# A buffer of its own for the small group's output in a fused attention and MLP kernel

## The chip, the cores and the metric

The kernel runs on one core of a Trainium2 chip. The metric is the device time of one execution in microseconds (us), median of several runs. The engines are named as the profile names them: PE is the matmul engine (PEld its weight loads), DVE the vector engine, ACT the scalar engine, POOL GpSimd, and SP the sync engine, which here issues DMA transfers only.

## The reference

```python
def _attn_ref(x, inducing):              # x: 4 x 12480 x 128, inducing: 32 x 128
    ...
    def mab(q, kv):
        s = scale * (q @ kv.transpose(0, 2, 1))
        s = s - s.max(-1, keepdims=True)
        a = np.exp(s)
        a /= a.sum(-1, keepdims=True) + 1e-09
        return a @ kv
    h = mab(I, x)                        # 32 rows per batch
    return mab(x, h)

def _moe_ref(x, w_in, w_out):            # 49920 x 128, 128 x 2048, 2048 x 128
    h = x @ w_in
    relu6 = np.clip(h + 3.0, 0.0, 6.0)
    g = h * relu6 / 6.0
    return g @ w_out
```

The output is `_moe_ref` of the attention's output, 49920 rows of 128 float32.

## The kernel before, in words

There are four batches b of 12480 tokens. Each is cut into groups: six of 2048 tokens (128 partitions times TG = 16) and a small last one of 192 tokens (96 partitions times 2). A large group has four chunks of 512 tokens, the small group is one chunk of 192: 25 chunks per batch (NCK), 100 in all. Phase a reads a batch's tokens and forms the 32 aggregated rows H. Phase c turns H into coefficients: since each token's attention output is a mix of the 32 rows of H, the first MLP matmul and the gate become products of attention weights, and the output is a linear part (BD) and a quadratic part (Cq). Phase b applies them to each chunk.

The order of the work is written out by hand. The main loop (from L970) goes over the 100 chunks t. For each it emits, in this order: the evacuation of the chunk before (`b_evac`), the spread of weights for the chunk six ahead (`b_spread`, an SP transfer into d), the product TD = TF * d for the next chunk (`b_prod`, L845, DVE), the first half of the features two chunks ahead (`b_base`, L827 on PE into bp, L834 on ACT into TF), at a group's turn its sum and nf (`b_f`, L751 on PE, L753 on DVE), the linear matmul that opens the chunk's PSUM bank op (`b_lin`, L856), then four rounds of quadratic matmuls from TF and TD into op (`b_quad`, L875). Between the rounds come the reciprocals r (`b_r`, L783 on PE, L787 on DVE), the packed weights of later groups (`b_pack`, L799 and L806; `b_e`, L735 and L741), and `bg`, which takes units of phases a and c of the next batch from a queue sorted by planned times. These units end with batch 3, which has no next batch. Among them are `a_T` (transposes L290, copy to xT L291), `a_s1` (L298 on PE, L304 on ACT), `a_agg` (L314 on PE, L327 on DVE, and the next load of x, L132 on POOL's queue), and `c_dG` on POOL (L516 waits for the newest TD, then L518 and L519).

`b_evac` (L884 to L902) multiplies op by r into an output buffer os (L892, DVE). At a group's first chunk (j == 0) it takes a new buffer from the pool osp, which has two (L107); when the group is full, SP writes it to DRAM in one transfer (L902), 1 MB for a large group. In the last two groups of the last batch each chunk is written by itself (L900). A buffer taken a second time waits until the write out of it has landed. op has two banks (psO), and the other matmuls share five banks (psF), so a matmul that needs a bank waits for its last reader.

The pool cst has one buffer per name or tag (L108). Its tag scr is used for d32 (L590) and r6 (L540), both before the first chunk of batch 0, and for junk in `count` (L950), which DVE runs in the last six chunks: `counts` at t == total - 6 (L1009), then L1011, and at t == total - 1 L988. Each is 2048 bytes per partition or less.

Of the kernel before, what the change touches and what calls it, by code (L numbers as in the profile page):

```python
# [9 lines left out]
FP32 = mybir.dt.float32  # L10
# [14 lines left out]
TG = 16  # L25
# [25 lines left out]
def kernel(  # L51
# [9 lines left out]
    P = nc.NUM_PARTITIONS  # L61
    B, N, C = x.shape
# [29 lines left out]
    with ExitStack() as es:  # L92
# [14 lines left out]
        osp = es.enter_context(tc.tile_pool(name="osp", bufs=2))  # L107
        cst = es.enter_context(tc.tile_pool(name="cst", bufs=1))  # L108
# [139 lines left out]
        def slots(n):  # L248

            return min(n, SL), max(n // SL, 1)  # L250
# [633 lines left out]
        def b_evac(b, c, op):  # L884
            g, j = chunks[c]
            t0, p, n = groups[g]
            st = S[b]
            if j == 0:
                st["os"] = osp.tile([P, TG, C], FP32, name="os")
            ot = st["os"]  # L890
            S_ = slots(n)[0]
            nc.vector.tensor_mul(  # L892
                ot[:p, j * S_ : (j + 1) * S_, :],
                op[:p, : S_ * C].rearrange("p (s c) -> p s c", c=C),
                r_all[:p, b, c, :S_].unsqueeze(2).to_broadcast([p, S_, C]),
            )
            r0 = b * N + t0
            rows = out[r0 : r0 + p * n, :].rearrange("(p i) c -> p i c", i=n)
            if b == B - 1 and g >= NGR - 2:
                nc.sync.dma_start(rows[:, j * S_ : (j + 1) * S_, :], ot[:p, j * S_ : (j + 1) * S_, :])  # L900
            elif (j + 1) * S_ == n:
                nc.sync.dma_start(rows, ot[:p, :n, :])  # L902
# [67 lines left out]
        for t in range(total):  # L970
# [4 lines left out]
            if evac:  # L975
                b_evac(*evac)
                evac = None
# [38 lines left out]

        assert not queue
        b_evac(*evac)
        verdict()

# [153 lines left out]
```

## Time and profile before

| | |
|---|---|
| median of three runs | 309.59 us |
| lowest and highest run | 309.18 and 311.05 us |
| the profiled execution | 310.18 us |
| its span, from the first to the last instruction | 308.3 us |
| mean granted PE clock in it | 0.987 |
| waits of SP's queue in L902 for os, total | 81.2 us in 25 waits |
| 1 MB writes of the output (23 of them), median to landing | 4.1 us |

A row of a timeline has the start in us from the span's start, the duration in us, the engine (SPq is SP's queue), the line, the operation, the tiles as out<-in, shapes as partitions x elements, the count of merged instructions, and in brackets the engine's idle time before it with the releaser that the profile infers. A row of waits has the waiting instruction, the releaser, total us, times, and the longest in us. A wait for several semaphores is put down to the one that came last by the profile; where that one had long been done, it was another, often a DMA. PE's matmuls are pipelined, so their modelled durations overlap, and distances between starts say more than durations.

### The profile page before, as it was taken

The page shows a single profiled execution, that of the slowest core. Times are in us where ns is not written, and L with a number is a line of the kernel's source. Part 1 is how long each engine was busy: PE and PEld are TensorE (multiplying, and loading weights), DVE is VectorE, ACT ScalarE, POOL GpSimd, SP SyncE. Part 2 cuts the span into 40 slices and gives each one's busy share as a digit, 9 for nine tenths or more (in the row PEclk, how much of TensorE's full clock was granted, in tenths as well). Part 3 has the DMA queues.
Part 4 walks back from the last instruction along what each step waited for, and adds up shares of the span by engine and source line. Part 5 has one row for each costly group of instructions (what it writes and reads, how often), then busy time and mean ns, then how long its engine had stood idle before and what let it go on. Part 6 is the DMA issues. An engine that isn't in the chain of part 4 may idle for free. (4 is left out here: it accounts for less than half of the span.)

```text
span 308.3 us, 9788 instructions
## 1 busy us (share of the span) xinstructions
PE 288.8 (94%) x3942; PEld 230.3 (75%) x3963; DVE 234.3 (76%) x499; ACT 224.9 (73%) x431; POOL 117.4 (38%) x234
## 2 busy tenths in 40 slices
PE   8978989999999899999998999998898999999992
PEld 3876577989888678777887977786687777777881
DVE  1567757887998578678897859788877885988893
ACT  3662769776968989668798899665696787777760
POOL 8460852431019995010097745000577760000000
PEclk9989999999999999999999999999999999999997
DMA  6999779699965547979628425256445565576753
GB/s 218 423 288 323 199 253 373 210 378 307 361 204 163 194 151 228 393 225 291 223 57 308 164 64 179 95 159 198 157 135 139 179 197 184 177 235 216 214 205 120
DMA packets 27441, 67.73 MB, mean 220 GB/s; under 512 B 5216, under 2 KB 20352, under 8 KB 21504
## 3 DMA queue, kind: packets, MB, share of 16 engines
q1 hardware_dynamic: 18784, 38.36, 38.4%
q0 software_dynamic: 8608, 28.71, 31.0%
q8 instruction: 32, 0.52, 0.7%
q14 instruction: 17, 0.14, 0.1%
HBM read 29.77 MB, written 25.56 MB: 179 GB/s over the span
## 5 line engine op out<-in xcount | busy, mean ns | idle before, releaser
L834 ACT ACTIVATE TF<-bp 128x512 bf16<-128x512 f32 (+1 forms) x200 | 115.6, 589 | 33.4 <-PE bp L827 17.9
L875 PE MATMUL op<-Cq,TF 128*128 128x128 bf16 (+1 forms) x784 | 104.7, 221 | 0.3
L875 PE MATMUL op<-Cq,TD 128*128 128x128 bf16 (+1 forms) x784 | 102.5, 219 | 0.0
L892 DVE TENSOR_TENSOR os<-op,r_all 128x512 f32<-128x512 f32 (+1 forms) x100 | 67.4, 674 | 23.5 <-PE op L875 18.9
L845 DVE TENSOR_TENSOR TD<-TF,d 128x1024 bf16<-128x1024 bf16 (+1 forms) x100 | 75.6, 756 | 4.3 <-ACT TF L834 3.3
L875 PEld LDWEIGHTS <-TF 128*128 128x128 bf16 (+1 forms) x784 | 55.1, 98 | 24.1 <-issue 12.7
L827 PE MATMUL bp<-xT,W 128*128 128x512 bf16 (+1 forms) x184 | 68.6, 375 | 2.2 <-DVE nf_all L753 1.0
L875 PEld LDWEIGHTS <-TD 128*128 128x128 bf16 (+1 forms) x784 | 60.3, 98 | 0.7 <-issue 0.2
L856 PE MATMUL op<-BD,nf 128*128 128x512 f32 (+1 forms) x100 | 52.3, 523 | 0.2 <-DVE os L892 0.2
L279 ACT CAST xb<-xr 128x512 bf16<-128x512 f32 (+1 forms) x70 | 45.3, 661 | 8.2 <-DMA xr<-in_x_dram 8.1
L291 DVE COPY xT<-pt 128x1024 bf16<-128x1024 bf16 (+1 forms) x56 | 34.0, 616 | 16.7 <-PE pt L290 15.8
L519 POOL TENSOR_TENSOR dg<-G 128x256 f32<-128x256 f32 x48 | 40.1, 836 | 0.0
L518 POOL TENSOR_TENSOR dg<-G 128x256 f32<-128x256 f32 x48 | 31.3, 653 | 14.6 <-ACT sq L526 10.1
L516 POOL COPY gate<-TD 128x1 bf16<-128x1 bf16 x48 | 11.7, 244 | 62.3 <-DVE TD L845 61.6
L526 ACT ACTIVATE sq<-dg 128x512 bf16<-128x512 f32 x48 | 30.3, 633 | 2.9 <-POOL dg L519 2.9
L314 PE MATMUL hnd<-xr,a 128*32 128x128 f32 x384 | 31.8, 229 | 0.6 <-ACT a L304 0.6
L290 PE MATMUL pt<-ident_b,xb 128*128 128x128 bf16 x392 | 30.9, 222 | 0.0
L603 PE MATMUL cp<-w_out_b,sq 128*128 128x128 bf16 x256 | 24.7, 219 | 2.5 <-ACT TF L834 1.3
L314 PEld LDWEIGHTS hnd<-xr,a 128*32 128x32 f32 x384 | 25.5, 111 | 1.7 <-ACT a L304 0.7
L783 PE MATMUL rp<-one,nf 128*128 128x4 f32 (+1 forms) x100 | 26.2, 264 | 0.5 <-ACT TF L834 0.5
L290 PEld LDWEIGHTS <-xb 128*128 128x128 bf16 x392 | 24.1, 99 | 2.8 <-issue 1.3
L806 ACT ACTIVATE dk<-pp 128x512 bf16<-128x512 f32 (+1 forms) x28 | 15.6, 556 | 12.3 <-PE pp L799 11.3
(127 smaller groups left out, 384.5 us busy)
## 6 DMA issues: line engine op xcount, KB each, us to landing
xr<-in_x_dram POOLq DMA_DIRECT2D x23, 1024.0 KB, 7.7
out_dram<-os SPq DMA_DIRECT2D x23, 1024.0 KB, 4.1
d<-dk SPq DMA_DIRECT2D x96, 128.0 KB, 4.4
xr<-in_x_dram POOLq DMA_DIRECT2D x2, 512.0 KB, 4.7
w_in_r<-in_moe_w_in_dram POOLq DMA_DIRECT2D x2, 512.0 KB, 10.7
w_out_r<-in_moe_w_out_dram POOLq DMA_DIRECT2D x1, 1024.0 KB, 14.1
out_dram<-os SPq DMA_DIRECT2D x4, 256.0 KB, 3.5
w_in_b<-in_moe_w_in_dram POOLq DMA_DIRECT2D x1, 512.0 KB, 7.7
```

The lines of the kernel that those rows point to most:

```text
L279: eng(xb[:p, lo:hi, :], xs[(b, g)][:p, lo:hi, :].bitcast(FP32))
L290: nc.tensor.transpose(pt[:, (i - lo) * p : (i - lo + 1) * p], xb[:p, i, :], ident_b[:p, :p])
L291: nc.vector.tensor_copy(st[("xT", g)][:, lo * p : hi * p], pt[:, : (hi - lo) * p])
L314: nc.tensor.matmul(st["hnd"][:M, :C], lhsT=a1[:p, i * M : (i + 1) * M], rhs=xs[(b, g)][:p, i, :], start=(g == 0 and i == 0), stop=(g == NG ...
L518: nc.gpsimd.tensor_sub(dg[:, 0], stepped(G2, jb, 0, 1, 0), stepped(G2, jb, 2, 0, 2))
L519: nc.gpsimd.tensor_sub(dg[:, 1], stepped(G2, jb, 1, -1, 0), stepped(G2, jb, 10, 0, 2))
L827: nc.tensor.matmul(bp[:, :w], lhsT=st["W"][:, k].rearrange("p m i -> p (m i)"), rhs=st[("xT", g)][:, j * w : (j + 1) * w],)
L834: nc.scalar.activation(st[("x", c)][:, k, :w], bp[:, :w], ACT.Exp, scale=scale)
L845: nc.vector.tensor_mul(u[:, :, :w], t[:, :, :w], d[:, :w].unsqueeze(1).to_broadcast([P, 2, w]))
L856: nc.tensor.matmul(op[:p, : S_ * C], lhsT=st[("nf", g)][:R, j * p : (j + 1) * p], rhs=st["BD"][:R, : S_ * C], start=True, stop=False, skip ...
L875: nc.tensor.matmul(op[:p, s * C : (s + 1) * C], lhsT=T[k][:, s * p : (s + 1) * p], rhs=st["Cq"][:, k, :], start=False, stop=(s == S_ - 1 a ...
L892: nc.vector.tensor_mul(ot[:p, j * S_ : (j + 1) * S_, :], op[:p, : S_ * C].rearrange("p (s c) -> p s c", c=C), r_all[:p, b, c, :S_].unsquee ...
```

## The change

The small group's output no longer takes a turn of the pool osp. It takes a tile of [128, 2, 128] float32, 1024 bytes per partition, in the pool cst under the tag scr, which it shares with d32, r6 and junk. The large groups go on taking turns of osp. The tile's name in the profile is ol.

```diff
             t0, p, n = groups[g]
             st = S[b]
             if j == 0:
-                st["os"] = osp.tile([P, TG, C], FP32, name="os")
+                if n == TG:
+                    st["os"] = osp.tile([P, TG, C], FP32, name="os")
+                else:
+                    st["os"] = cst.tile([P, n, C], FP32, name="ol", tag="scr")
             ot = st["os"]
```

## The prediction

> **What bounds the kernel now.** I read the page first, then DVE's waits, and then the timelines of DVE, SP and PE around the three places where a batch's small group is followed by the next batch. From the page:
>
> ```profile
> span 308.3 us, 9788 instructions
> PE 288.8 (94%) x3942; PEld 230.3 (75%) x3963; DVE 234.3 (76%) x499; ACT 224.9 (73%) x431; POOL 117.4 (38%) x234
> ```
>
> The reader is to see that PE is busy for 288.8 of 308.3 us. DVE, whose waits the change alters, idles 74 us, nearly all of it hidden: a wait on DVE is worth only what PE loses by it. DVE's waits have two entries that stand out because each is one occurrence alone:
>
> ```profile
> DVE os L892 <- PE rp L783: 2.2, 1, 2.2
> DVE os L892 <- PE pp L799: 1.8, 1, 1.8
> ```
>
> Columns are total us, times, longest. The named releasers can't be the true ones: an evacuation of op into os needs neither rp nor pp. So I looked at what else was due. First the end of batch 0 (DVE and one ACT row, then SP; the last two rows are the landing of that one SP transfer, and DVE's semaphore wait on L892):
>
> ```profile
> 129.02 0.69 DVE L291 COPY xT<-pt 128x1024 bf16<-128x1024 bf16 x1
> 129.46 0.60 ACT L834 ACTIVATE TF<-bp 128x512 bf16<-128x512 f32 x1 [0.51 <-PE bp L827]
> 131.92 0.69 DVE L892 TENSOR_TENSOR os<-op,r_all 128x512 f32<-128x512 f32 x1 [2.21 <-PE rp L783]
> 132.53 0.68 DVE L845 TENSOR_TENSOR TD<-TF,d 128x1024 bf16<-128x1024 bf16 x1
> 133.13 0.68 DVE L753 CUSTOM_DVE_ANT_0 nf<-e,sp 128x512 fp32r<-128x512 f32 x1
> ...
> 125.14 0.34 SPq L902 DMA_DIRECT2D out_dram<-os  x1
> ...
> DMA to landing us min/median/max: 6.7/6.7/6.7
> ...
> L892 DVEq EVENT_SEMAPHORE  x1: 50/50/50, 131.8 to 131.8; - x1
> ```
>
> The 1 MB write of batch 0's group 5 is issued at 125.14 and lands 6.7 later, at 131.8. That is when DVE's semaphore is passed, and 0.1 later the first os of batch 1 starts. The small group had taken the other buffer, so batch 1 needs group 5's at once. DVE stood still for 2.21 us with work queued behind: the TD product and the nf reduction.
>
> **The change part by part.** No arithmetic, shape, transfer or issue order changes. The small group's buffer comes from the one-buffer tag scr, so the two os buffers turn six times per batch instead of seven, and batch b+1's group 0 gets the buffer of batch b's group 4.
>
> *Removed, batch 0 to 1.* What PE lost:
>
> ```profile
> 126.53 0.38 PE L827 MATMUL bp<-xT,W 128*128 128x512 bf16 x1
> 126.98 0.28 PE L875 MATMUL op<-Cq,TF 128*128 128x128 bf16 x2
> 127.10 0.28 PE L875 MATMUL op<-Cq,TD 128*128 128x128 bf16 x2
> ...
> 128.93 0.28 PE L875 MATMUL op<-Cq,TD 128*128 128x128 bf16 x2
> ...
> 132.08 0.38 PE L827 MATMUL bp<-xT,W 128*128 128x512 bf16 x1
> 132.67 0.49 PE L856 MATMUL op<-BD,nf 128*128 128x512 f32 x1 [0.21 <-DVE os L892]
> 133.00 0.29 PE L875 MATMUL op<-Cq,TF 128*128 128x128 bf16 x2
> 133.27 0.28 PE L875 MATMUL op<-Cq,TD 128*128 128x128 bf16 x2
> 133.87 0.55 PE L298 MATMUL s<-I_T,xT 128*128 128x32 bf16 x16 [0.32 <-DVE nf_all L753]
> ...
> 198.28 0.28 PE L875 MATMUL op<-Cq,TD 128*96 128x128 bf16 x2
> 198.40 0.55 PE L298 MATMUL s<-I_T,xT 128*128 128x32 bf16 x16
> ```
>
> Undisturbed, L827 to the first TF matmul (past L856) takes 126.98 - 126.53 = 0.45, TF to TD 127.10 - 126.98 = 0.12, and TD to L298 198.40 - 198.28 = 0.12: together 0.69. Here 132.08 to 133.87 takes 1.79. PE waited for the op bank that os frees, then for TD (133.27, just after TD's end at 132.53 + 0.68 = 133.21), then for the bank that nf frees (133.13 + 0.68 = 133.81). All three are queued behind the stalled os, so the stall costs PE 1.79 - 0.69 = 1.10 us.
>
> What is late next? The os needs the op whose last matmul is done at 128.93 + 0.28 = 129.21, and DVE is free at 129.02 + 0.69 = 129.71; so it can start 131.92 - 129.71 = 2.21 earlier. TD then starts near 130.3; its TF is ready at 129.46 + 0.60 = 130.06. So PE's own instruction stream is what ends last there, and I take the whole 1.10. Its other end is zero, if something else fills the same place.
>
> *Removed, batches 1 to 2 and 2 to 3:*
>
> ```profile
> 202.13 0.28 PE L875 MATMUL op<-Cq,TD 128*128 128x128 bf16 x2
> 202.49 0.69 DVE L892 TENSOR_TENSOR os<-op,r_all 128x512 f32<-128x512 f32 x1 [0.56 <-PE op L875]
> ...
> 257.72 0.34 SPq L902 DMA_DIRECT2D out_dram<-os  x1
> ...
> DMA to landing us min/median/max: 4.0/4.0/4.0
> ...
> 261.84 0.69 DVE L892 TENSOR_TENSOR os<-op,r_all 128x512 f32<-128x512 f32 x1 [1.83 <-PE pp L799]
> ...
> 262.67 0.58 PE L856 MATMUL op<-BD,nf 128*128 128x512 f32 x1
> 264.47 0.50 PE L856 MATMUL op<-BD,nf 128*128 128x512 f32 x1
> 266.15 0.58 PE L856 MATMUL op<-BD,nf 128*128 128x512 f32 x1
> ...
> 270.26 0.58 PE L856 MATMUL op<-BD,nf 128*128 128x512 f32 x1
> 271.83 0.58 PE L856 MATMUL op<-BD,nf 128*128 128x512 f32 x1
> 273.48 0.58 PE L856 MATMUL op<-BD,nf 128*128 128x512 f32 x1
> ```
>
> Batch 2's first os starts at 202.49; its matmuls end at 202.13 + 0.28 = 202.41. It could start at most 0.08 earlier: nothing. Batch 3's waits for the write issued at 257.72 (257.72 + 4.0 = 261.7) and stalls 1.83. Batch 3 has no background work, so its groups repeat. Chunks 2 and 3 of group 0 take 264.47 - 262.67 = 1.80 and 266.15 - 264.47 = 1.68; those of group 1 take 271.83 - 270.26 = 1.57 and 273.48 - 271.83 = 1.65. PE lost 0.23 + 0.03 = 0.26.
>
> *Added.* The small os now waits for the last user of scr: in batch 0 for work finished before the first chunk, in batches 1 and 2 for a write one batch old, and in batch 3 for the counts' junk on DVE itself. The last is the only close one; it stands at the end of the kernel, with nothing queued behind but the last write:
>
> ```profile
> 302.24 0.28 PE L875 MATMUL op<-Cq,TD 128*96 128x128 bf16 x2
> ...
> 302.36 0.08 DVE L951 DVE_READ_ACCUMULATOR junk<-r_all 128x1 f32 x1
> 302.55 0.42 DVE L892 TENSOR_TENSOR os<-op,r_all 96x256 f32<-96x256 f32 x1
> ```
>
> The junk is done at 302.44, the matmuls at 302.52, so the wait is covered by 0.08 us. Uncovered, it costs about what lies between a semaphore passed and the next start, 0.1 us in the row at 131.8 and 131.92; a gain is excluded, since the matmuls come last anyway. I take 0. SP and POOL issue the same transfers in the same order; they only move earlier with the work.
>
> *Sum.* 1.10 + 0.00 + 0.26 = 1.36 us. The profiled execution took 310.18, so 308.82 on its scale. The median of the runs, 309.59, lies 0.59 below it: 309.59 - 1.36 = 308.23. I say 308.2.
>
> [...] What made the first stall long is the landing time, 6.7 against 4.0 us for the same 1 MB. The transfer engines were full there (columns: us; busy by engine; clock; DMA share and GB/s):
>
> ```profile
> 126.00:132.00 6.00, 5.93 (x81) 4.83 (x82) 3.54 (x9) 4.78 (x10) 0.18 (x1) 1.00 1.00 371
> ```
>
> [...] The row has 6.7 with every engine busy, and I go by the row.
>
> **The rivals.**
>
> *A. The write lands early.* If 6.7 us is a crossing of loads peculiar to the profiled execution, and other executions have the 4.0 of batch 2's end, it lands at 125.14 + 4.0 = 129.1, before 129.71, and the first stall isn't there. Only 0.26 is left: 309.59 - 0.26 = 309.3. Against it: the order of issue is fixed and the share is 1.00.
>
> *B. The gain is absorbed.* ACT (73%) and POOL pace stretches of batches 1 and 2; PE that comes earlier may wait there instead. Then some 0 to 0.5 us are left: 309.3. Against it: ACT's and POOL's work is released by PE's and DVE's own progress, and moves with it.
>
> *C. Slower: DVE's work falls against POOL's.*
>
> ```profile
> 236.88 0.61 POOL L518 TENSOR_TENSOR dg<-G 128x256 f32<-128x256 f32 x1 [0.51 <-ACT sq L526]
> 236.97 1.08 DVE L845 TENSOR_TENSOR TD<-TF,d 128x1024 bf16<-128x1024 bf16 x1
> ```
>
> A TD product beside POOL's dg takes 1.08 instead of 0.68 (132.53), 0.40 more. A shifted phase may stretch more of them in batches 1 and 2. It decides once 4 more stretched ones (1.6) lie on PE's path; with 8, the time is 309.59 - 1.36 + 3.2 = 311.4. [...] Against it: DVE has slack there, and as many may part as meet.
>
> *D. The change doesn't do what it says*, and the first os of a batch still waits for a write: 309.6.
>
> **How the numbers follow.** Chances: forecast 0.58, A 0.10, B 0.22, C 0.06, D 0.04. About 1% (3.1 us) is what a measurement of this kernel can tell from no change; only C with 11 or more stretched products on the path passes that upwards, and only a gain more than twice the sum downwards. So faster by over 1% 0.03, within 1% 0.94, slower 0.03. The range: the lowest run shown is 0.4 below the median, and the gain may be 0.6 larger if PE's lead spares a later stall: 307.2. Upwards it takes in A, B and D at 309.6 with 0.6 of scatter: 310.2. It leaves out most of C. The forecast's own range is 307.6 to 308.9.
>
> **What would show it.** In the changed trace DVE's two lone waits of 2.2 and 1.8 are gone; the small os carries a name of its own; the first os of batches 1 and 3 starts as soon as DVE is free; L827 to L298 after batch 1's second chunk takes near 0.7; chunk 2 of batch 3 takes 1.57. If these hold and the span is not about 1.4 shorter, B is right, and PE's idle time must be found later. If the landing is near 4 in the trace after, A gains. If more TD products take over 1 us than now, C does. The prediction is wrong if the stalls go and PE's steps there stay as they are.

## The result and the profile after

| | before | after |
|---|---|---|
| median | 309.63 us (308.82 to 311.52, 8 runs) | 307.75 us (307.58 to 309.0, 8 runs) |
| ratio | | 0.9936, 95% interval 0.991 to 0.9963 |
| profiled execution and its span | 310.18 and 308.3 us | 307.74 and 306.0 us |

The kernel became 0.6% faster, within the 1% named in the prediction; the interval leaves out 1, and a second series further down gives the same ratio. The ratio of `twice` further down leaves out two of its four runs, which took over 1.5% longer than its fastest. The medians differ by 1.88 us, the two profiled executions by 2.44, and the prediction was 1.36. So there are two questions: whether the 1.36 us came from where the prediction put them, and where the rest comes from.

The page after, its first two lines:

```profile
span 306.0 us, 9804 instructions
PE 286.6 (94%) x3963; PEld 228.6 (75%) x3963; DVE 235.0 (77%) x499; ACT 224.8 (73%) x431; POOL 117.2 (38%) x234
```

DVE's waits after (waiting line and releaser, total us, times, longest):

```profile
DVE os L895 <- PE op L875: 20.0, 55, 1.0
```

L895 is L892 of before, three lines further down. The two lone entries of 2.2 and 1.8 us are gone, and this is the only entry of os that is left. DVE's timeline at the start of batch 1 and of batch 3:

```profile
128.03 0.69 DVE L291 COPY xT<-pt 128x1024 bf16<-128x1024 bf16 x1
128.64 0.68 DVE L895 TENSOR_TENSOR os<-op,r_all 128x512 f32<-128x512 f32 x1
129.24 0.68 DVE L845 TENSOR_TENSOR TD<-TF,d 128x1024 bf16<-128x1024 bf16 x1
129.83 0.68 DVE L753 CUSTOM_DVE_ANT_0 nf<-e,sp 128x512 fp32r<-128x512 f32 x1
...
256.96 0.37 DVE L895 TENSOR_TENSOR ol<-op,r_all 96x256 f32<-96x256 f32 x1
257.25 0.68 DVE L845 TENSOR_TENSOR TD<-TF,d 128x1024 bf16<-128x1024 bf16 x1
258.23 0.69 DVE L895 TENSOR_TENSOR os<-op,r_all 128x512 f32<-128x512 f32 x1 [0.31 <-PE op L875]
```

The first os of batch 1 now follows the copy before it at once, TD and nf follow it, and batch 3's waits only for its own matmuls. PE's timeline after:

```profile
128.51 0.40 PE L856 MATMUL op<-BD,nf 128*128 128x512 f32 x1
131.09 0.38 PE L827 MATMUL bp<-xT,W 128*128 128x512 bf16 x1
131.12 0.58 PE L856 MATMUL op<-BD,nf 128*128 128x512 f32 x1
131.54 0.29 PE L875 MATMUL op<-Cq,TF 128*128 128x128 bf16 x2
131.66 0.28 PE L875 MATMUL op<-Cq,TD 128*128 128x128 bf16 x2
131.78 0.38 PE L298 MATMUL s<-I_T,xT 128*128 128x32 bf16 x9
133.79 0.58 PE L856 MATMUL op<-BD,nf 128*128 128x512 f32 x1
...
258.48 0.40 PE L856 MATMUL op<-BD,nf 128*128 128x512 f32 x1
260.58 0.59 PE L856 MATMUL op<-BD,nf 128*128 128x512 f32 x1
262.16 0.58 PE L856 MATMUL op<-BD,nf 128*128 128x512 f32 x1
263.80 0.59 PE L856 MATMUL op<-BD,nf 128*128 128x512 f32 x1
```

From L827 to L298 it takes 131.78 - 131.09 = 0.69 us, where the kernel before took 1.79: 1.10 less. In batch 3, chunk 2 takes 1.58 and chunk 3 1.64 instead of 1.80 and 1.68: 0.26 less. Both are what the prediction worked out. From the first chunk on, all other chunks keep their distances within 0.03 us. So 1.36 of the 2.3 us between the spans lie at the two stalls. Most of the rest lies ahead of the first chunk, where the change touches nothing: its L856 starts at 47.17 us before and at 46.21 after, 0.96 us apart. In this view of 4 us (busy time by engine in the order PE, PEld, DVE, ACT, POOL; the last three columns are the granted clock, the DMA share and GB/s) before comes first and after second:

```profile
20.00:24.00 4.00, 3.88 (x58) 3.85 (x59) 3.02 (x7) 2.16 (x4) 0.30 (x1) 0.59 1.43 192
```

```profile
20.00:24.00 4.00, 3.62 (x74) 3.52 (x75) 3.42 (x8) 2.95 (x6) 0.41 (x1) 1.00 1.43 187
```

The reader is to see the granted clock: 0.59 in the profiled execution before, 1.00 in the one after.

### The profile page after: what moved, and what is told of

The parts are those of the page before. It is cut to its first block, busy times and chain, and to the rows that moved or that the text cites. A ratio compares the mean times of both kernels' runs of the same rounds, so it can differ in the third digit from the quotient of the medians.

```text
span 306.0 us, 9804 instructions
## 1 busy us (share of the span) xinstructions
PE 286.6 (94%) x3963; PEld 228.6 (75%) x3963; DVE 235.0 (77%) x499; ACT 224.8 (73%) x431; POOL 117.2 (38%) x234
## 5 line engine op out<-in xcount | busy, mean ns | idle before, releaser
L895 DVE TENSOR_TENSOR os<-op,r_all 128x512 f32<-128x512 f32 x96 | 65.9, 686 | 20.7 <-PE op L875 20.0
L827 PE MATMUL bp<-xT,W 128*128 128x512 bf16 (+1 forms) x200 | 74.8, 375 | 2.2 <-DVE nf_all L753 1.0
L856 PE MATMUL op<-BD,nf 128*128 128x512 f32 (+1 forms) x100 | 52.5, 525 | 0.0
L314 PE MATMUL hnd<-xr,a 128*32 128x128 f32 x384 | 31.0, 226 | 0.6 <-ACT a L304 0.6
L290 PEld LDWEIGHTS <-xb 128*128 128x128 bf16 x392 | 23.3, 98 | 3.8 <-ACT xb L279 2.1
L314 PEld LDWEIGHTS hnd<-xr,a 128*32 128x32 f32 x384 | 24.7, 109 | 1.8 <-ACT a L304 0.7
```

The costliest lines, as they stand in the source:

```text
L290: nc.tensor.transpose(pt[:, (i - lo) * p : (i - lo + 1) * p], xb[:p, i, :], ident_b[:p, :p])
L314: nc.tensor.matmul(st["hnd"][:M, :C], lhsT=a1[:p, i * M : (i + 1) * M], rhs=xs[(b, g)][:p, i, :], start=(g == 0 and i == 0), stop=(g == NG ...
L827: nc.tensor.matmul(bp[:, :w], lhsT=st["W"][:, k].rearrange("p m i -> p (m i)"), rhs=st[("xT", g)][:, j * w : (j + 1) * w],)
L856: nc.tensor.matmul(op[:p, : S_ * C], lhsT=st[("nf", g)][:R, j * p : (j + 1) * p], rhs=st["BD"][:R, : S_ * C], start=True, stop=False, skip ...
L895: nc.vector.tensor_mul(ot[:p, j * S_ : (j + 1) * S_, :], op[:p, : S_ * C].rearrange("p (s c) -> p s c", c=C), r_all[:p, b, c, :S_].unsquee ...
```

## The experiments

For each profile below, the loss at batch 1 is measured in one way. In PE's timeline I take the distance of L856 of batch 1's second chunk to L856 of its fourth, and subtract that of the changed kernel, 133.79 - 128.51 = 5.28 us. For batch 3 it is the distance from its third to its fifth chunk, less 263.80 - 260.58 = 3.22.

**The kernel before once more** (no edit).

> The kernel before, unchanged, profiled once more. The two profiled executions before and after differ by 0.98 us already ahead of the first chunk's output matmul (47.17 against 46.21 us), where the change touches nothing, and in the first one the granted clock was 0.59 between 20 and 24 us. Theory: that part belongs to the execution and not to the kernel; in this trace it will be another amount (0 to 1 us), the granted clock between 20 and 24 us another, while every distance from the first chunk on is the same within 0.05 us, the 1.10 and 0.26 us losses at batches 1 and 3 among them. Rival: the first 47 us of the kernel before are slower by 1 us in every execution, so something in the change shortens them; then the first chunk's matmul starts at 47.2 again. Time: same, ratio 1.000 within 0.003.

Measured: 310.61 us (309.63 to 312.33, 11 runs), ratio 1.0035 (1.0014 to 1.0057). The same program, timed against itself, lies 0.35% off, outside the 0.3% that was expected, and its interval leaves out 1: single intervals of this size don't decide. Its mean clock was 0.993 or more in 1 of 11 runs, against 23 of the 35 beside it. Rows of its PE and DVE timelines and of two windows:

```profile
46.35 0.59 PE L856 MATMUL op<-BD,nf 128*128 128x512 f32 x1
128.68 0.40 PE L856 MATMUL op<-BD,nf 128*128 128x512 f32 x1
134.61 0.58 PE L856 MATMUL op<-BD,nf 128*128 128x512 f32 x1
...
130.65 0.69 DVE L892 TENSOR_TENSOR os<-op,r_all 128x512 f32<-128x512 f32 x1 [1.76 <-DMA out_dram<-os]
...
20.00:24.00 4.00, 3.53 (x73) 3.36 (x72) 3.34 (x8) 2.95 (x6) 0.84 (x2) 1.00 1.43 187
222.60:226.10 3.50, 3.50 (x25) 2.82 (x25) 1.50 (x3) 2.13 (x4) 2.24 (x6) 0.51 0.43 96
```

The first chunk starts at 46.35, not at 47.17, so at least 0.82 of the 0.96 us ahead of it belong to the execution, as expected. This execution was granted half the clock later, at 222.6 to 226.1, and lost 1.3 us there. And here the profile names the true releaser of batch 1's wait, the write out of os. One part of the expectation was wrong: the loss at batch 1 is not fixed. The distance is 134.61 - 128.68 = 5.93, a loss of 0.65 where the first profile had 1.10. The write landed 6.2 us after its issue, not 6.7, and DVE waited 1.76 us, not 2.21.

**One batch at a time.** `own_b0` gives only batch 0's small group the buffer of its own, `own_b2` only batch 2's.

```diff
-                if n == TG:
+                if n == TG or b != 0:      # own_b2: b != 2
```

> Only batch 0's small group gets the buffer of its own. Theory: the two stalls are separate, so the step at batch 1 (1.10 us of PE) goes and the 0.26 at batch 3 stays: from the first chunk on 1.10 us less than before, the waits of 1.8 us at batch 3's first os still there. Rival (what PE gains at batch 1 is caught later, and only both together shorten the end): less than 0.5. Time: 308.5, ratio 0.9965.

Measured: 308.2 us (308.01 to 309.62, 12 runs), ratio 0.9959 (0.9942 to 0.9976). The distance at batch 1 is that of the changed kernel, 135.01 - 129.73 = 5.28, while batch 3's wait of 1.82 us is still there:

```profile
129.73 0.40 PE L856 MATMUL op<-BD,nf 128*128 128x512 f32 x1
135.01 0.59 PE L856 MATMUL op<-BD,nf 128*128 128x512 f32 x1
...
260.97 0.69 DVE L895 TENSOR_TENSOR os<-op,r_all 128x512 f32<-128x512 f32 x1 [1.82 <-PE pp L799]
```

> Only batch 2's small group gets the buffer of its own. Theory: 0.26 us less than before from the first chunk on, all of it in the chunks after batch 3's first os; the 2.2 us wait at batch 1 stays. Rival: the stall at batch 3 is the 1.8 us that DVE's wait lists, and the end comes 1.8 earlier. Time: 309.4, ratio 0.999; by the rival 307.8, 0.994.

Measured: 309.71 us (309.26 to 310.68, 12 runs), ratio 0.9996 (0.9981 to 1.0012). The distance at batch 3 is 3.22, as with the change. So the two stalls are separate, each gain is kept to the end, and at batch 3 PE lost 0.26 of a 1.83 us wait, not the whole. At batch 1 this execution lost more than either before it:

```profile
129.52 0.40 PE L856 MATMUL op<-BD,nf 128*128 128x512 f32 x1
136.35 0.58 PE L856 MATMUL op<-BD,nf 128*128 128x512 f32 x1
...
132.40 0.69 DVE L895 TENSOR_TENSOR os<-op,r_all 128x512 f32<-128x512 f32 x1 [2.66 <-PE op L875]
```

A wait of 2.66 us, a distance of 6.83, a loss of 1.55.

**Group 5 written in pieces.**

```diff
-            if b == B - 1 and g >= NGR - 2:
+            if g == NGR - 2 or (b == B - 1 and g >= NGR - 2):
```

> Buffers as before; group 5 of every batch is written out chunk by chunk, 256 KB each, so three quarters of it are on their way before the last chunk is evacuated. Theory (what stalls DVE is the landing of the write, not the number of buffers): the last piece is issued at 125.1 and a piece of this size took 2.5 to 4.0 us at the end of the kernel before, so it lands near 128.5 and both stalls go: from the first chunk on 1.2 to 1.37 us less, as with the change. Rival A of the prediction in another form (full transfer engines delay the last piece as much as the 1 MB write): it lands near 131, and less than 0.5 us is gained at batch 1. Nine more issues on SP cost 0.34 us each of SP's queue, which delays d; by the theory that is hidden. Time: 308.3, ratio 0.996.

Measured: 312.78 us (310.09 to 314.35, 12 runs), ratio 1.0081 (1.0052 to 1.0109). The expectation failed at batch 1. The last piece is 256 KB, and it landed 8.1 us after its issue, where the four of this size at the end of the kernel before took 5.3, 4.0, 2.9 and 2.5 (an SP row and its landing, a POOL row of an x load and its landing, and DVE's wait):

```profile
125.28 0.34 SPq L900 DMA_DIRECT2D out_dram<-os  x1
...
DMA to landing us min/median/max: 8.1/8.1/8.1
...
123.65 0.53 POOL L132 DMA_DIRECT2D xr<-in_x_dram  x1 [1.77 <-PE bp L827]
...
DMA to landing us min/median/max: 9.5/9.5/9.5
...
133.47 0.69 DVE L892 TENSOR_TENSOR os<-op,r_all 128x512 f32<-128x512 f32 x1 [3.61 <-DMA out_dram<-os]
```

The load issued at 123.65 landed at 133.2, and the piece behind it at 133.4, so the piece's small size didn't bring it down early. But the load itself took 9.5 us here, and 5.3 to 6.6 in the nine profiles with the same load in which the write was one transfer: the pieces slowed the load too, and why they did isn't shown. DVE waited 3.61 and PE lost 2.51. At batch 3, where no load is under way, the pieces took the loss away (distance 3.22). The rest of the slowdown against the profile before is a stretch at half clock from 225.5 us, which cost 1.3 us; one at 20 us is in both (a mean clock of 0.59 over 20 to 24 us in each).

**A load of x held back.** In batch 2's phase a, ahead of the load that stood in front of the write:

```diff
+                if b == 2 and g == 4:
+                    hold = cst.tile([P, 1], BF16, name="gate")
+                    nc.gpsimd.tensor_copy(hold[:, :], latest[0][:, 0, 0:1])
                 load_next(b, g)
```

> Buffers and writes as in the kernel before; one load of x, 1 MB for batch 3's group 2, is held back by a copy on POOL that waits for a TD product of batch 1 (the load was issued at 123.50, just ahead of group 5's write at 125.14, and is needed some 20 us later or more). Theory (the stall at batch 1 is that write's landing, and its landing is late because the transfers issued ahead of it fill the engines): the write lands 4.0 to 4.7 us after its issue, DVE's wait at batch 1 falls from 1.8 to 2.7 us to 0 to 0.3, and PE gets back 0.65 to 1.5 there; the 0.26 at batch 3 stays. Rival (the landing is late for another reason, say the spread of weights on SP's own queue): the wait stays near 2. Time: 308.7, ratio 0.9965.

Measured: 308.26 us (307.67 to 310.48, 12 runs), ratio 0.9948 (0.9928 to 0.9969). The buffers are those of the kernel before, and the stall is gone (SP, its landing, DVE):

```profile
125.31 0.34 SPq L905 DMA_DIRECT2D out_dram<-os  x1
...
DMA to landing us min/median/max: 4.0/4.0/4.0
...
129.79 0.68 DVE L895 TENSOR_TENSOR os<-op,r_all 128x512 f32<-128x512 f32 x1
```

The held load was issued at 131.7 instead of 123.5, and the load before it (at 120.6) and the spreads of d stayed. With one load less ahead of it, the same 1 MB write lands in 4.0 us and DVE doesn't wait; the distance at batch 1 is 5.28, and batch 3's wait of 1.83 is as before. So the stall at batch 1 takes two things: two buffers turning seven times, and the load issued just ahead of the write. Removing either removes it.

**A second turn of the pool**, meant to lengthen the wait.

```diff
                 st["os"] = osp.tile([P, TG, C], FP32, name="os")
+                if n < TG:
+                    osp.tile([P, TG, C], FP32, name="os")
```

> The small group takes two turns of the pool (the second buffer is never written), so the next batch's first os gets the small group's own buffer and waits for the small write, which is issued 2.6 us after group 5's and landed 1.39 (batch 1), 1.7 (batch 2) and 1.35 us (batch 3) later than it. Theory: what PE loses is DVE's wait less a fixed cover. In the profiles so far batch 1's wait and PE's loss were 2.21 and 1.10, 1.76 and 0.65, 2.66 and 1.55, 3.61 and 2.50 us, always 1.11 apart; batch 3's 1.83 and 0.26, 1.57 apart. So the losses become the new waits less 1.11 and less 1.57: with waits of 3.6 and 3.2, 2.5 and 1.6 us; batch 2, with a wait of 1.6 and a cover not known, 0 to 0.5. In all 2.8 to 3.2 us more than before from the first chunk on. Rival (PE loses a share of the wait, half of it at batch 1 and a seventh at batch 3): 1.8 and 0.45, 0.9 more than before. Time: 312.6, ratio 1.009; by the rival 310.6, 1.003.

Measured: 309.32 us (308.55 to 312.92, 12 runs), ratio 0.9977 (0.9951 to 1.0002). The edit did nothing: the buffer that is never written was not waited for, and the next os still waited for group 5's write (it started at 132.59, the write landed at 132.5, and the small group's own write at 133.6). It is one more profile of the kernel before: a wait of 2.51 at batch 1 and a distance of 6.68, a loss of 1.40. Neither theory was tested by it, but the sum of profiles was. Batch 1's waits and losses are now 1.76 and 0.65, 2.21 and 1.10, 2.51 and 1.40, 2.66 and 1.55, 3.61 and 2.51 (pieces). All five differ by 1.10 to 1.11 us.

**One output buffer for the large groups**, in the changed kernel.

```diff
-        osp = es.enter_context(tc.tile_pool(name="osp", bufs=2))
+        osp = es.enter_context(tc.tile_pool(name="osp", bufs=1))
```

> The changed kernel with one output buffer for the large groups instead of two: now every group's first os waits for the write of the group before. Theory (wait less cover): in batch 3 such a write is issued 0.7 us after the last os of a group has begun and takes 4.0 to 5.2 to land, and the next os would begin 1.6 to 2.0 after the last: waits of 2.8 to 3.9, less 1.57 of cover 1.2 to 2.3 for each of five boundaries; in the batches with more transfers 2 to 4 for each of 18. In all 45 to 80 us: 355 to 385, ratio 1.15 to 1.25. Rival (the wait is hidden as long as DVE has slack, and DVE is busy 76%): under 15 us, ratio under 1.05.

Measured: 379.71 us (373.19 to 386.99, 4 runs), inside the expected 355 to 385, though these runs also had a lower mean granted clock (0.90 to 0.94), so the sum itself proves little. One boundary at full clock, DVE and PE:

```profile
333.23 0.69 DVE L895 TENSOR_TENSOR os<-op,r_all 128x512 f32<-128x512 f32 x1 [3.61 <-DMA out_dram<-os]
...
330.15 0.39 PE L856 MATMUL op<-BD,nf 128*128 128x512 f32 x1
333.98 0.49 PE L856 MATMUL op<-BD,nf 128*128 128x512 f32 x1 [1.38 <-DVE os L895]
335.86 0.50 PE L856 MATMUL op<-BD,nf 128*128 128x512 f32 x1
337.54 0.58 PE L856 MATMUL op<-BD,nf 128*128 128x512 f32 x1
```

The three chunks take 337.54 - 330.15 = 7.39 us; the same three chunks of a group of batch 3 in the changed kernel take 263.80 - 258.48 = 5.32. PE lost 2.07 of a 3.61 us wait. The cover is 1.54, as at batch 3's first os (1.83 - 0.26 = 1.57). A share of the wait, a seventh, would have been 0.5. The same reckoning elsewhere in this trace, where the granted clock stayed at 1.00, gives 1.54 at the next boundary (wait 3.86, loss 2.32) and 1.10 at batch 1's first os (wait 2.69, loss 1.59), the cover found there before. At six other boundaries it is 1.24 to 1.94 five times, and 3.15 once (wait 3.39, loss 0.24). So the cover belongs to the place and has to be read there.

**The changed kernel once more** (no edit).

> The changed kernel, unchanged, once more, in turn with the kernel before. In the profiles so far single stretches of 3.41 us at half the granted clock, at 20.7 or at 222.7 us, cost 0.8 to 1.3 us each, and they come in some executions of the kernel before and not in others. Theory: they fall on either kernel alike, so the two differ by the stalls alone (1.1 to 1.5 at batch 1 by the landing, 0.26 at batch 3): ratio 0.9945 to 0.996. Rival: the changed kernel has fewer of them: ratio under 0.994, and its runs with a mean clock under 0.992 are a fifth of those of the kernel before or less.

Measured: 307.92 us (307.67 to 310.16, 11 runs), ratio 0.9937 (0.9913 to 0.9962). The distances are again 5.28 and 3.22. The ratio is the one found first; it lies just below the theory's 0.9945 to 0.996, though its interval takes that in. Four of its 11 runs had a mean clock under 0.992, and eight of the 28 runs of the kernel before beside it: the rival's condition on the clock isn't met, and a lower mean clock comes with both kernels alike as far as these counts go.

**Group 5 of batches 0 to 2 written twice**, in the kernel before (`twice`) and in the changed one (`twice_own`).

```diff
                 nc.sync.dma_start(rows, ot[:p, :n, :])
+                if g == NGR - 2:
+                    nc.sync.dma_start(rows, ot[:p, :n, :])
```

> The kernel before, but group 5's output of batches 0 to 2 is written out twice, the same rows with the same values, so that its buffer comes free one transfer later. (Swap didn't lengthen the wait: a second buffer that is never written is not waited for, and that run was the kernel before once more.) Theory (PE loses DVE's wait less a fixed cover of 1.11 us at batch 1 and 1.53 to 1.57 at batch 3): the second 1 MB lands 2.5 to 4.5 us after the first, so the waits are 4.5 to 7 at batch 1 and 4.3 to 6.3 at batch 3, and the losses are these less the covers: 3.4 to 6 and 2.8 to 4.8, against 0.65 to 1.55 and 0.26 before. At batch 2, where the first write landed just when it was needed, a wait of 2.5 to 4.5 less a cover of 1 to 2 gives 1 to 3. In all 6 to 12 us more than before: 316 to 322, ratio 1.02 to 1.04. Rival (PE loses a share of the wait, half at batch 1, a seventh at batch 3): 2.3 to 3.5 and 0.6 to 0.9, ratio 1.005 to 1.013.

Measured: 329.7 us (324.94 to 332.25, 4 runs), ratio 1.0522 (1.043 to 1.0613), far above what was expected. SP issued the second write only when the first had landed (at batch 0's end the two at 125.32 and 132.84, the first landing after 7.5 us), so DVE waited 11.46, 5.48 and 5.64 us. Part of the loss is a lower granted clock (0.50 for 10 us at batch 1, and lower also after the waits at batches 2 and 3), so the cover can't be read from it. Neither the theory nor the rival is tested by this run.

> The changed kernel with the same doubled writes. Theory (the write costs nothing but by its buffer): with the buffer of its own, the next batch's first os waits for nothing, and batch 1's second group, which now takes group 5's buffer, starts 10 us later; the 3 MB more of traffic are hidden: 307.7 to 308.3, ratio 0.993 to 0.996. Rival (the added traffic itself delays loads of x or the spread of weights): 1 to 4 us more than the changed kernel, and twice's loss is then not the buffer's.

Measured: 310.83 us (310.36 to 313.9, 10 runs), ratio 1.003 (0.999 to 1.007). The distances at both places are 5.28 and 3.22: the buffer's stall is gone, as the theory has it. But the kernel is some 3 us slower than the changed one, as the rival has it, and the place is on SP, DVE and PE:

```profile
131.38 0.34 SPq L907 DMA_DIRECT2D out_dram<-os  x1
131.77 0.55 SPq L815 DMA_DIRECT2D d<-dk  x1
...
140.15 0.69 DVE L845 TENSOR_TENSOR TD<-TF,d 128x1024 bf16<-128x1024 bf16 x1 [3.18 <-DMA d<-dk]
...
140.90 0.28 PE L875 MATMUL op<-Cq,TD 128*128 128x128 bf16 x2 [1.77 <-DVE TD L845]
```

While SP waited from 124.6 to 131.4 for the first write, the spreads of d queued behind it. Those issued from 131.8 to 134.8 then took 7.6 to 8.5 us to land, against 3.3 to 5.8 for those of the changed kernel issued from 127.2 to 132.6. TD waited 3.18 us for one of them, and PE lost 2.2 us there in one chunk. In this profile a stretch at half clock from 224.5 us cost another 1.3. So of what `twice` lost, the waits of DVE are the buffer's; the 2.2 us here are late spreads of d, and how they divide between SP's queue and the added traffic isn't shown.

## Why the prediction was right, step by step

*What bounds the kernel, and who was waited for.* Right. The profile named rp and pp as releasers; the landing times named the write, and three later profiles (`before_again`, `swap` and `pieces`) name it outright.

*Batch 0 to 1, 1.10 us.* Right in its mechanism and, for this pair of profiles, to the hundredth; PE's own stream was what ended last, and all of it was kept. What the prediction did not see is that 1.10 is one draw. Over four executions with the old buffers the landing was 6.2, 6.7, 7.0 and 7.1 us and the loss 0.65, 1.10, 1.40 and 1.55: the landing less 5.6, within 0.1. This is the term that was mis-sized, and it was too small. In the five other profiles in which the same write stands behind the same load, it took 7.1 us three times (`twice_own` and the two of the changed kernel), 7.2 (`own_b0`) and 7.5 (`twice`). So the usual landing was near 7.1, worth a loss of about 1.5 (an estimate from these pairs), and the profile behind the prediction had the second shortest of nine. That the profile after gives 1.10 to the hundredth says nothing about the usual size: it is subtracted from the same profile before.

*Batch 1 to 2, nothing; batch 2 to 3, 0.26.* Right: 0.00 and 0.26, and the second is shown apart by `own_b2`. Batch 3's first os doesn't start as soon as DVE is free, as the prediction's signs had it, but 0.31 us later, when its matmuls are done.

*The added wait.* Right. The last rows after, on DVE:

```profile
300.00 0.08 DVE L954 DVE_READ_ACCUMULATOR junk<-r_all 128x1 f32 x1
...
300.19 0.42 DVE L895 TENSOR_TENSOR ol<-op,r_all 96x256 f32<-96x256 f32 x1
```

From the junk's end (300.08) to ol it takes 0.11 us, as from 302.44 to 302.55 before.

*Rival A* (the write lands early) was wrong for this kernel and right as a mechanism: `late_x` made the write land in 4.0 us and the stall vanished. The write at the end of batch 2, where no load of x is left, also took 4.0 us; just behind a load the rows have 6.2 to 7.5, and the sum had to go by those.

*Rival B* (absorbed) fell: no chunk after the two places gave any of it back. *Rival C* fell: 15 TD products took over 1 us before and 15 after, and the median stayed at 682 ns. (To slow the kernel by 1% it needed 12 such products and not 11: 11 x 0.40 - 1.36 = 3.04 us, short of 3.1.) *Rival D* fell with the tile's own name ol and with the first os of batch 1, which waits for nothing.

*The size of the whole.* 1.88 us between the medians against 1.36. The sum of the four executions' losses runs from 0.91 to 1.81, and the usual landing gives about 1.5 + 0.26 = 1.8. Stretches of some 3.4 us at half clock cost 0.82 to 1.3 us each where the traces have them, and some runs of either kernel have a mean clock under 0.992, so runs of like clock say more. Of those with a mean clock of 0.993 or more, the changed kernel's second series has a median of 307.87 us (7 runs) against 309.73 (14 runs of the kernel before), 1.86 apart; `own_b0` lies 1.49 below the kernel before and `own_b2` 0.29. These agree with a loss near 1.5 at batch 1 rather than 1.10. They don't prove it: `swap`, in effect the kernel before, lies 0.45 below it by the same reckoning, and the timed runs leave no trace of their landings. So the forecast of 308.2 came within 0.5 us of the measured 307.75 with the right mechanism and, as far as the record shows, with one term some 0.4 us too small. No version in these runs beats the changed kernel; three shared buffers were not tried.

## What to carry to other kernels

A wait on an engine that is not the bound cost, in these runs, the wait less a cover (1.10 us at batch 1, 1.57 at batch 3), the work that the bound can do before it needs what is queued behind. Read the cover off two chunks' distances with and without the stall, at the place itself, and don't take a share of the wait. Where a small odd item takes a turn in a pool of two, the next large item gets the buffer of the large item just before it (here waits of 2.21 and 1.83 us); look for single long waits at such seams, and check a named releaser against the landings of transfers. A stall that ends with a landing had no fixed price here (0.65 to 1.55 us in four executions): two or three profiles of the same kernel give its spread.

## What the runs showed of the hardware

The landing of group 5's write depended on what had been issued just before it: its 1 MB to DRAM took 4.0 us without a load of x close ahead (the ends of batches 1 and 2, and `late_x`) and 6.2 to 7.5 behind a 1 MB load issued 1.6 us earlier, and the last 256 KB of `pieces` took 8.1 us behind one. The granted clock fell to about 0.5 in stretches of some 3.4 us: at 20 us in the first profile of the kernel before, at 222 us in the second, at neither in the two of the changed kernel, which have 1.00 there. With the first, the first chunk started 0.82 to 0.96 us later (at 47.17, against 46.35 and 46.21 without), and the second cost 1.3 us, each nearly as much as the whole change. In both profiles PE was idle for 1.8 us of the 3.4 us before the fall. The kernel before at its first fall (us, then busy us by engine in the order PE, PEld, DVE, ACT, POOL, then clock, DMA share and GB/s), and the same kernel once more at its fall:

```profile
17.30:20.70 3.40, 1.59 (x34) 1.32 (x32) 2.22 (x4) 1.75 (x3) 3.00 (x5) 1.00 1.10 312
20.70:24.10 3.40, 3.40 (x48) 3.36 (x46) 2.36 (x5) 1.98 (x4) 0.00 (x0) 0.50 1.49 180
```

```profile
219.20:222.66 3.46, 1.69 (x24) 1.04 (x22) 2.51 (x6) 2.85 (x6) 3.46 (x7) 1.00 0.91 326
222.66:226.07 3.41, 3.41 (x25) 2.73 (x25) 1.50 (x3) 2.07 (x4) 2.15 (x6) 0.50 0.44 97
```

The idle time is not enough for a fall: the changed kernel's profile has the same gap on PE at 18 to 19.6 us (1.56 us, against 1.58) and a granted clock of 1.00 after it. What decides whether one execution meets a fall and the next does not isn't shown.
